# First group's attention in pairs of heads, with the low word of the weights on GpSimd

## The chip, the cores and the metric

One core of one Trainium2 chip runs the whole program. The metric is the device time of one execution in microseconds; lower is better. Three executions of the kernel before took 725.34, 726.88 and 729.34 us, a median of 726.88.

## The reference

Causal attention over 2 batches of 8 heads with 576 positions and head size 64, with a bias from cumulative sums; then two feed-forward layers over the 1152 tokens.

```python
scores = scale * (q @ k.T);  cum = cumsum(max(s, 0))
bias = -(cum[q] - cum[k])
scores = where(causal, -1e9, scores + min(bias, 0))
attn = softmax(scores);  x = attn @ v          # (1152, 512)
h = x @ w_in                                   # layer 1: 512 -> 2048
g = where(h > 0, h, exp(min(h, 0)) - 1);  x = g @ w_out
p = domain_probs / sum(domain_probs)           # layer 2: 4 experts, 512 -> 1024 -> 512
out = sum_e p[:, e] * (max(x @ w1[e], 0) @ w2[e])
```

The weights of layer 1 arrive as 64-bit floating-point numbers. The kernel takes them as pairs of 32-bit words and puts each number together from its high and its low word.

## The kernel before

**Tokens** come in three groups of 256, 448 and 448. For the first group the program runs its attention, then layer 1, then layer 2. The attention of the second group is cut into small parts, which are fed as background work into the end of the first group's layer 1 and into its layer 2. Then comes layer 1 of the second group with the attention of the third beside it, layer 1 of the third, and layer 2 of both.

**Layer 1** has 16 units of weights. A unit is 128 columns of `w_in` and 128 rows of `w_out`, 1 MB in 64-bit form. `layer1` (L648) makes one slot per unit: `up1` (four products into a PSUM bank, then the activation function in two ScalarE operations, L680 and L683, and one VectorE operation, L684, which writes the tile `gt`), and `down1` (four products, L663), two slots later. `slot` (L596) also calls the background work and `advance` (L573). `advance` decodes ahead (`AHEAD`), fetches and prepares the units that follow (layer 2's first unit is unit 16; `prepare`, L95, splits it into a high part on ScalarE, L99, and a low part on VectorE, L83).

**Decoding.** A unit has two halves, 32 halves in all. `fetch_halves` (L118) fetches a half (512 KB) by SP's queue into whatever buffer is free in a list of places (`turn`, L106): the tiles `wu`, `gt`, `yh`, `yl`, `raw`, `xa` and `ox` that later work will use. The first 16 halves find free places; each later one waits for a decode to free its place. `decode_halves` (L131) does per half one ScalarE operation on the high word (L146), one ScalarE operation on the low word (L148, into `z`, two buffers), and two VectorE operations that join them (L149, L151). After the second half of a unit, GpSimd's queue writes the decoded unit to DRAM (`w_dec`, L154), from where the later groups read it.

**Attention of the first group** (`attention_first`, L236) takes all 8 heads at once. `cum_sums` makes the cumulative sums, `cum_parts` writes their rows to DRAM (`rows_d`) for the later groups, `cum_columns` their columns. The scores of all heads (16 products, L277, and 32 for the bias, L283 and L285) fill six PSUM banks. `probabilities` takes a bank: per head a VectorE operation (L295, mask and row extreme) and an exponential on ScalarE (L297). `normalise` scales four heads, half on ScalarE (L304), half on VectorE (L305). `transposes` goes through PSUM and a ScalarE copy (L313), `values` multiplies by v, and a ScalarE copy (L322) writes `x_first`. Calls of `decode_halves` stand between: `DEC` has the number of halves that are decoded by each.

**Order.** The code is written in one sequence; a scheduler of the tile library then sets each engine's own order, by data dependences and its own estimates. Each engine and each DMA queue takes its instructions strictly in that order, so one that waits holds up all behind it. SP's queue carries nearly all loads, and the second group's first loads are tied to stand behind the last weight fetch (`late`, L525).

## Time and profile before

| | us |
|---|---|
| median of three runs | 726.88 |
| the profiled execution's own time | 726.64 |
| its span, first to last instruction | 724.8 |
| TensorE busy (share of the span) | 693.3 (96%) |
| VectorE busy | 559.1 (77%) |
| ScalarE busy | 371.7 (51%) |
| GpSimd busy | 13.6 (2%) |

Busy time is an average over stages that differ: a TensorE that is busy for 96% can still stand idle for a large part of one stage. So the stages are read apart, by windows of time. In a timeline a row begins with the start and the duration; a bracket at its end gives the idle time of the engine ahead of it and what ended that. Instructions of one engine may overlap a little, so the step from one start to the next is the better measure of a rate. PE is TensorE, DVE is VectorE, ACT is ScalarE, POOL is GpSimd; SPq is the queue that SP issues DMAs from.

### The profile page before, as it was taken

Reading aid. Unit: us, or ns where it says so; the run is one execution under the profiler, and the core shown is the slowest. Engines: PE = TensorE matmul, PEld = TensorE weight load, DVE = VectorE, ACT = ScalarE, POOL = GpSimd, SP = SyncE. Lnnn points to the kernel's source line nnn. Section 1 sums busy time; section 2 is a strip of 40 time slices with the busy share of each in tenths; the row PEclk is TensorE's granted clock in tenths of the full one; section 3 lists DMA queues with packets and bytes.
Section 4 is the critical chain, followed back from the end, with each engine's and each line's share of the span. In section 5 each row is a group of like instructions: output and inputs, shape, how many; then the busy total and the mean of one; then the engine's idle time right before and its main releaser. Section 6 shows DMA issues by size and latency. Waiting matters only on the chain.

```text
span 724.8 us, 10238 instructions
## 1 busy us (share of the span) xinstructions
PE 693.3 (96%) x3626; PEld 591.7 (82%) x3626; DVE 559.1 (77%) x1142; ACT 371.7 (51%) x777; POOL 13.6 (2%) x33
## 2 busy tenths in 40 slices
PE   5489789999999999999999999999999999999997
PEld 4378678888878888778899988888888888888886
DVE  4678659988875998886795549988888887887765
ACT  3978658776765878666744333222222222332320
POOL 2011000000000000000000000000000000000000
PEclk9599999999999999999999999999999999999999
DMA  8769994667556453441552000111111111111002
GB/s 325 301 237 368 327 319 160 207 198 216 167 188 203 166 158 108 145 141 59 213 222 88 30 0 1 59 58 59 59 58 59 59 58 59 58 59 59 0 1 101
DMA packets 41954, 96.98 MB, mean 134 GB/s; under 512 B 5200, under 2 KB 18704, under 8 KB 41904
## 3 DMA queue, kind: packets, MB, share of 16 engines
q1 hardware_dynamic: 39440, 87.69, 36.5%
q0 software_dynamic: 2304, 8.39, 2.9%
q8 instruction: 28, 0.46, 0.3%
q10 hardware_dynamic: 160, 0.26, 0.1%
q14 instruction: 22, 0.18, 0.1%
HBM read 85.32 MB, written 11.01 MB: 133 GB/s over the span
## 4 chain that ended last, share of the span: by engine, by line
PE 87%; ACT 4%; DMA 3%; DVE 3%; SPq 2%; issue 1%; DVEq 0%; ACTq 0%
PE acc L562 38%; PE up L562 16%; PE att L882 11%; PE up L882 8%; PE att L517 3%; PE att L490 3%; PE acc L663 2%; PE up L676 2%; PE att L445 1%; PE att L438 1%; SPq L370 1%; PE att L440 1%; DMA wu<-in_w 1%; DMA raw<-in_w 1%; DMA q<-in_qT 1%
## 5 line engine op out<-in xcount | busy, mean ns | idle before, releaser
L562 PE MATMUL acc<-w,h 128*128 128x512 f32 x672 | 172.0, 392 | 0.0
L562 PEld LDWEIGHTS acc<-w,h 128*128 128x128 f32 x672 | 126.1, 188 | 23.0 <-ACT h L892 0.2
L83 DVE TENSOR_TENSOR wu<-raw,wu 128x1024 fp32r<-128x1024 f32 x64 | 78.2, 1222 | 22.9 <-ACT wu L99 21.7
L562 PE MATMUL acc<-gt,wu 128*128 128x448 f32 x384 | 88.6, 373 | 0.0
L630 DVE SCALAR_TENSOR_TENSOR ox<-acc,pr,ox 128x512 f32<-128x512 f32 x105 | 78.6, 748 | 10.7 <-PE acc L562 8.6
L892 ACT ACTIVATE h<-c 128x448 fp32r<-128x448 f32 x48 | 27.4, 574 | 114.7 <-DVE c L898 114.7
L99 ACT ACTIVATE wu<-raw 128x1024 fp32r<-128x1024 f32 x64 | 67.5, 1055 | 22.4 <-PE acc L562 16.5
L562 PEld LDWEIGHTS acc<-gt,wu 128*128 128x128 f32 x384 | 70.1, 188 | 8.7 <-issue 2.6
L882 PE MATMUL att<-S,top 128*128 128x448 f32 x288 | 66.3, 365 | 0.0
L882 PEld LDWEIGHTS att<-S,top 128*128 128x128 f32 x288 | 54.0, 188 | 6.7 <-issue 0.2
L562 PE MATMUL acc<-wu,gt 128*128 128x512 f32 x192 | 56.4, 409 | 0.0
L562 PE MATMUL up<-yh,wu 128*128 128x256 f32 x256 | 52.6, 287 | 0.0
L893 DVE SCALAR_TENSOR_TENSOR h<-c,h 128x448 fp32r<-128x448 f32 x48 | 29.9, 624 | 18.7 <-ACT h L892 18.7
L882 PE MATMUL up<-x2a,top 128*128 128x448 f32 x192 | 44.2, 366 | 0.0
L562 PEld LDWEIGHTS up<-yh,wu 128*128 128x128 f32 x256 | 41.9, 190 | 2.7 <-issue 1.7
L562 PE MATMUL up<-xa,wu 128*128 128x448 f32 x192 | 43.6, 371 | 0.0
L562 PE MATMUL up<-ox,wu 128*128 128x448 f32 x192 | 42.1, 368 | 0.7 <-DVE e L688 0.7
L480 ACT ACTIVATE p<-p,nm 128x384 f32<-128x384 f32 (+4 forms) x56 | 34.5, 617 | 13.6 <-DVE nm L475 13.4
L680 ACT ACTIVATE e<-up 128x448 f32<-128x448 f32 (+1 forms) x48 | 23.5, 490 | 33.7 <-PE up L562 31.7
L882 PEld LDWEIGHTS up<-x2a,top 128*128 128x128 f32 x192 | 35.9, 188 | 4.8 <-ACT p L907 0.5
L562 PEld LDWEIGHTS up<-ox,wu 128*128 128x128 f32 x192 | 36.0, 188 | 4.6 <-DVE e L688 1.1
L892 ACT ACTIVATE h<-up 128x448 fp32r<-128x448 f32 x16 | 8.8, 547 | 58.1 <-PE up L882 58.1
(186 smaller groups left out, 1217.8 us busy)
## 6 DMA issues: line engine op xcount, KB each, us to landing
raw<-in_w SPq DMA_DIRECT2D x41, 512.0 KB
raw<-w_dec SPq DMA_DIRECT2D x32, 512.0 KB
raw<-in_w SPq DMA_DIRECT2D x16, 1024.0 KB
w_dec<-wu POOLq DMA_DIRECT2D x16, 512.0 KB, 6.7
k<-in_kT SPq DMA_DIRECT2D x16, 288.0 KB
xa<-in_w SPq DMA_DIRECT2D x6, 512.0 KB
ox<-in_w SPq DMA_DIRECT2D x6, 512.0 KB
cbp<-cum_d SPq DMA_DIRECT2D x16, 144.0 KB
```

What stands on the lines that cost most here:

```text
L83: DVE.tensor_tensor(out=lo, in0=x, in1=hi.bitcast(F32), op=ALU.subtract)
L99: ACT.activation(t[:, 0], x, AF.Copy)
L480: ACT.activation(p, p, AF.Exp, bias=nm, scale=-1.0, accum_out=sm)
L490: PE.transpose(pt[:cb[c + 1] - cb[c], m, :], p[:, cb[c]:cb[c + 1]], ident)
L517: PE.matmul(o[64 * j:64 * j + 64, qs:nq], job["v"][:n, c, 64 * j:64 * j + 64], job["pt"][:n, j, c, qs:nq], start=c == 0, stop=c == n_c - 1)
L562: PE.matmul(o, a[m], b[n], start=first and i == 0, stop=last and i == 2)
L630: DVE.scalar_tensor_tensor(out=o_sb, in0=o, scalar=pr[:, i, e:e + 1], in1=o_sb, op0=ALU.mult, op1=ALU.add)
L663: PE.matmul(o, t[:, 512 + 128 * c:640 + 128 * c], gt, start=k == 0, stop=k == NAB - 1)
L680: ACT.activation(e, o, AF.Exp)
L882: PE.matmul(bank, tops[q][:, m, op, cs], x[:, n, c], start=first and c + i == 0, stop=c == 1 and i == 2, skip_group_check=True)
L892: ACT.activation(h[:, 0, u, cs], c, AF.Relu)
L893: DVE.scalar_tensor_tensor(out=h[:, 1, u, cs], in0=c, scalar=0.0, in1=h[:, 0, u, cs].bitcast(F32), op0=ALU.max, op1=ALU.subtract)
```

## The change

1. `attention_first` works by pairs of heads (`hp` = 0 to 3). Each head has one PSUM bank for both its chunks. Scores of three pairs are made first, those of the fourth after the first pair's probabilities; then probabilities, normalising, transposes and values of the pairs follow each other as a pipeline. q and k are loaded in two halves each.
2. `normalise` scales everything on VectorE.
3. The low word of a half is taken by a multiplication on GpSimd instead of ScalarE's copy with a scale.
4. `DEC` is 1, 2, 3, 4 instead of 2, 5, 8, 10, and `AHEAD` 6 instead of 8: fewer halves are decoded during the attention, and less far ahead afterwards.
5. `cum_parts` and `cum_columns` are called in slot 3 of layer 1 instead of within and right after the attention.

```diff
-DEC = [2, 5, 8, 10]
-AHEAD = 8
+DEC = [1, 2, 3, 4]
+AHEAD = 6
...
-            ACT.activation(z, low.bitcast(U32), AF.Copy, scale=7.49 / 2 ** 32)
+            POOL.tensor_scalar(z, low.bitcast(U32), 7.49 / 2 ** 32, None, op0=ALU.mult)
...
     def cum_sums():
-        SP.dma_start(out=s_sb, in_=s)
...
+    def cum_parts():
+
         ACT.dma_start(out=cum_d, in_=cum)
-
-    def cum_parts():
-
...
-        cum_sums()
-        SP.dma_start(out=qkv[:, 0], in_=qT[0, :, 0:n].rearrange("(c p) n -> p c n", p=128))
-        SP.dma_start(out=qkv[:, 1], in_=kT[0, :, 0:n].rearrange("(c p) n -> p c n", p=128))
-        fetch_halves(2)
+        SP.dma_start(out=s_sb, in_=s)
+        for c in (0, 2):
+            for i, t in enumerate((qT, kT)):
+                SP.dma_start(out=qkv[:, i, c:c + 2], in_=t[0, 128 * c:128 * c + 256, 0:n]
+                             .rearrange("(c p) n -> p c n", p=128))
+        fetch_halves(1)
...
+        chunks = [(0, 128), (128, 256)]
+        banks = {}
+
+        def scores(hp):
+            for j in range(2):
+                h = 2 * hp + j
+                banks[h] = ps(f"acc{h % 4}", 1) if h < 4 or h > 5 else ps("up", 2)
...
+        def probabilities(hp):
+            for j in range(2):
+                h = 2 * hp + j
+                for i, (d0, d1) in enumerate(chunks):
+                    p = pp[h][:, d0:d0 + d1]
+                    nm = sb([128, 1], "nm", 8)
+                    DVE.tensor_tensor_reduce(p, banks[h][:, d0:d0 + d1], mask[:, S - d1:],
+                                             -1.0 / SC, 3.0e38, ALU.add, ALU.min, nm)
+                    ACT.activation(p, p, AF.Exp, bias=nm, scale=-1.0, accum_out=sm[:, i, h:h + 1])
+
+        def normalise(hp):
+            r = sm[:, :, 2 * hp:2 * hp + 2]
             DVE.tensor_scalar(r, r, 1e-9, None, op0=ALU.add)
             DVE.reciprocal(r, r)
-            for h in range(h0, h0 + 4):
-                ACT.activation(pp[h][:, 128:], pp[h][:, 128:], AF.Copy, scale=sm[:, 1, h:h + 1])
-                DVE.tensor_scalar(pp[h][:, :128], pp[h][:, :128], sm[:, 0, h:h + 1], None,
-                                  op0=ALU.mult)
...
+            for h in (2 * hp, 2 * hp + 1):
+                for i, (d0, d1) in enumerate(chunks):
+                    p = pp[h][:, d0:d0 + d1]
+                    DVE.tensor_scalar(p, p, sm[:, i, h:h + 1], None, op0=ALU.mult)
...
+        for hp in range(3):
+            scores(hp)
         probabilities(0)
+        decode_halves(DEC[0])
+        scores(3)
         probabilities(1)
-        decode_halves(DEC[0])
+        normalise(0)
+        transposes(0)
         probabilities(2)
+        normalise(1)
+        transposes(1)
+        values(0)
+        decode_halves(DEC[1])
         probabilities(3)
...
-    cum_columns(0, 4)
-    cum_columns(1, 4)
...
+    def sums_hook(k):
+        if k == 3:
+            cum_parts()
+            cum_columns(0, 4)
+            cum_columns(1, 4)
+
+    yacc = layer1(0, x_first, background, sums_hook)
```

What the scheduler makes of it is read from each engine's order.

ScalarE's order from the write of the cumulative sums to the first exponentials (L297 before, L301 after the change), where the sums' rows, the decoding and the attention meet. `bias` first holds `s` and later a row of ones. Before:

```order
L192 DMA cum_d<-cum 16x576
L202 ACTIVATE rows<-cum 16x576
L148 ACTIVATE z_246<-wu 128x512
L205 DMA rows_d<-rows 16x1152
L262 ACTIVATE cump<-cum 16x256
L262 ACTIVATE cumm<-cum 16x256
L199 DMA rows_d<-bias 16x576 x2
L202 ACTIVATE rows<-cum 16x576
L146 ACTIVATE wu<-wu 128x512
L148 ACTIVATE z_251<-wu 128x512
L205 DMA rows_d<-rows 16x1152
L297 ACTIVATE k_137,sm_142<-k_137,nm 128x128 x2
```

With the change:

```order
L193 DMA cum_d<-cum 16x576
L200 ACTIVATE rows<-cum 16x576
L203 DMA rows_d<-rows 16x1152
L263 ACTIVATE cump<-cum 16x256
L263 ACTIVATE cumm<-cum 16x256
L197 DMA rows_d<-bias 16x576 x2
L301 ACTIVATE k_138,sm_143<-k_138,nm 128x128
L301 ACTIVATE k_138,sm_143<-k_138,nm 128x256
```

The low words (L148) are gone, the second `rows` (L202, now L200) has moved behind nine exponentials, and the DMAs of `cum_d`, of the first `rows` and of the ones have stayed ahead of the first exponential.

VectorE's order in layer 1, two slots: L149 and L151 are the two joining operations of a half, L684 (L692 with the change) writes a slot's gated tile `gt`. Before, from the third gated tile on:

```order
L684 SCALAR_TENSOR_TENSOR gt<-up,e 128x256
L149 SCALAR_TENSOR_TENSOR wu<-wu,z_466 128x512
L151 SCALAR_TENSOR_TENSOR wu<-xa,wu 128x512
L149 SCALAR_TENSOR_TENSOR wu<-wu,z_506 128x512
L151 SCALAR_TENSOR_TENSOR wu<-ox,wu 128x512
L684 SCALAR_TENSOR_TENSOR gt<-up,e 128x256
L149 SCALAR_TENSOR_TENSOR wu<-wu,z_496 128x512
L151 SCALAR_TENSOR_TENSOR wu<-xa,wu 128x512
L149 SCALAR_TENSOR_TENSOR wu<-wu,z_532 128x512
L151 SCALAR_TENSOR_TENSOR wu<-ox,wu 128x512
L684 SCALAR_TENSOR_TENSOR gt<-up,e 128x256
```

With the change, from the first gated tile on:

```order
L692 SCALAR_TENSOR_TENSOR gt<-up,e 128x256
L213 COPY cum_t_97<-att 128x16
L149 SCALAR_TENSOR_TENSOR wu<-wu,z_381 128x512
L149 SCALAR_TENSOR_TENSOR wu<-wu,z_387 128x512
L151 SCALAR_TENSOR_TENSOR wu<-gt,wu 128x512
L151 SCALAR_TENSOR_TENSOR wu<-yh,wu 128x512
L692 SCALAR_TENSOR_TENSOR gt<-up,e 128x256
L149 SCALAR_TENSOR_TENSOR wu<-wu,z_404 128x512
L149 SCALAR_TENSOR_TENSOR wu<-wu,z_413 128x512
L151 SCALAR_TENSOR_TENSOR wu<-yl,wu 128x512
L151 SCALAR_TENSOR_TENSOR wu<-raw,wu 128x512
L692 SCALAR_TENSOR_TENSOR gt<-up,e 128x256
```

There are two halves a slot in both. Ahead of the first gated tile stand 4 halves' L149 with the change, where 11 stood before.

ScalarE's order near the end of the first layer 1: L680 and L683 (L688 and L691) are a slot's activation function, L426, L427 and L429 (L434, L435 and L437) split the next group's q and k, which wait for its loads, and L99 is the high part of layer 2's units. Before, from the activation function of the 14th slot on:

```order
L99 ACTIVATE wu<-raw 128x1024
L680 ACTIVATE e<-up 128x256
L683 ACTIVATE e<-e 128x256
L99 ACTIVATE wu<-raw 128x1024
L680 ACTIVATE e<-up 128x256
L683 ACTIVATE e<-e 128x256
L426 ACTIVATE qs<-pt 128x128
L427 ACTIVATE kh<-pt 128x128
L429 ACTIVATE qb<-pt 64x128
L480 ACTIVATE p,sm<-p,nm 128x128
```

With the change, from that of the 15th slot on:

```order
L688 ACTIVATE e<-up 128x256
L691 ACTIVATE e<-e 128x256
L99 ACTIVATE wu<-raw 128x1024
L434 ACTIVATE qs<-pt 128x128
L435 ACTIVATE kh<-pt 128x128
L437 ACTIVATE qb<-pt 64x128
L488 ACTIVATE p,sm<-p,nm 128x128
L688 ACTIVATE e<-up 128x256
L99 ACTIVATE wu<-raw 128x1024
L691 ACTIVATE e<-e 128x256
```

The first of layer 2's units stood ahead of the 14th slot's activation function and stands behind the 15th's; the second stands between the two operations of the 16th.

## Rows read from the trace of the kernel before

**Rows 1.** Busy time by windows, the sum of 105 to 724.8 us.

```profile
sum 619.80, PE 614.99 PEld 525.89 DVE 489.94 ACT 297.80 POOL 0.00; mean PE 205.00 PEld 175.30 DVE 163.31 ACT 99.27 POOL 0.00
```

**Rows 2.** Timeline of PE: start, duration, instruction, records, idle before.

```profile
6.43 4.34 PE L277 MATMUL acc<-pt 64*128 64x128 f32 x23 [6.43 <-DMA pt<-in_kT]
...
36.73 0.82 PE L312 MATMUL att<-ident,q 128*128 128x128 f32 x6
...
61.25 1.89 PE L676 MATMUL up<-xf,wu 128*128 128x256 f32 x8
...
64.70 1.89 PE L676 MATMUL up<-xf,wu 128*128 128x256 f32 x8
...
82.43 3.68 PE L676 MATMUL up<-xf,wu 128*128 128x256 f32 x8 [3.76 <-DVE gt L684]
...
104.95 0.47 PE L562 MATMUL up<-yh,wu 128*128 128x256 f32 x1
```

**Rows 3.** Timeline of ACT up to the first exponential.

```profile
8.43 0.67 ACT L148 ACTIVATE z<-wu 128x512 int32<-128x512 uint32 x1 [2.73 <-DMA wu<-in_w]
...
13.16 0.68 ACT L202 ACTIVATE rows<-cum 16x576 fp32r<-16x576 f32 x1 [3.46 <-DMA rows_d<-rows]
...
16.65 0.40 ACT L297 ACTIVATE k<-k,nm 128x128 f32<-128x128 f32 x1 [1.69 <-DVE nm L295]
```

**Rows 4.** Timeline of DVE: gated tiles (L684) and joining operations.

```profile
43.40 0.75 DVE L684 SCALAR_TENSOR_TENSOR gt<-up,e 128x256 f32<-128x256 f32 x2
...
65.39 0.42 DVE L684 SCALAR_TENSOR_TENSOR gt<-up,e 128x256 f32<-128x256 f32 x1
65.73 0.68 DVE L151 SCALAR_TENSOR_TENSOR wu<-xa,wu 128x512 int32<-128x512 int32 x1
66.33 0.69 DVE L149 SCALAR_TENSOR_TENSOR wu<-wu,z 128x512 int32<-128x512 int32 x1
...
69.06 0.42 DVE L684 SCALAR_TENSOR_TENSOR gt<-up,e 128x256 f32<-128x256 f32 x1
```

**Rows 5.** Timeline of SP's issues, then of ACT, 60 to 116 us.

```profile
62.81 5.33 SPq L127 DMA_DIRECT2D raw<-in_w  x3
...
90.17 0.33 SPq L93 DMA_DIRECT2D raw<-in_w  x1
...
80.84 0.31 ACT L429 ACTIVATE qb<-pt 64x128 fp32r<-64x128 f32 x1 [5.21 <-DMA pt<-in_qT]
...
96.85 1.06 ACT L99 ACTIVATE wu<-raw 128x1024 fp32r<-128x1024 f32 x1 [2.67 <-DMA raw<-in_w]
```

**Rows 6.** Busy time by windows, 90 to 105 us: PE, PEld, DVE, ACT, POOL, PEclk, DMA share, GB/s.

```profile
90.00:105.00 15.00, 12.96 (x62) 10.54 (x61) 8.95 (x27) 7.89 (x24) 1.06 (x2) 1.00 1.06 316
```

**Rows 7.** Groups by line and form, 0 to 105 us: busy us, mean ns | idle us before.

```profile
L148 ACT ACTIVATE z<-raw 128x512 int32<-128x512 uint32 x9 | 6.1, 698 | 1.3 <-DVE wu L149 1.3
...
L83 DVE TENSOR_TENSOR wu<-raw,wu 128x1024 fp32r<-128x1024 f32 x2 | 2.5, 1225 | 4.9 <-ACT wu L99 4.9
...
L295 DVE CUSTOM_DVE_ANT_0 k<-acc,mask 128x256 f32<-128x256 f32 x4 | 1.5, 419 | 0.0
...
L295 DVE CUSTOM_DVE_ANT_0 k<-acc,mask 128x128 f32<-128x128 f32 x6 | 1.4, 285 | 0.0
...
L305 DVE TENSOR_SCALAR k<-k,sm 128x128 f32<-128x128 f32 x6 | 1.4, 297 | 0.1
```

**Rows 8.** Timeline of POOL and DVE, 1.5 to 5.2 us.

```profile
1.50 0.29 POOL masks.py:199 TENSOR_SCALAR_AFFINE_SELECT ident<-ident 128x128 f32<-128x128 f32 x1
...
3.12 0.19 POOL L259 CAST ones<-ident 16x16 fp32r<-16x16 f32 x1
...
3.24 1.34 DVE L191 TENSOR_TENSOR_SCAN cum<-bias 16x576 f32<-16x576 f32 x1 [3.24 <-ACT bias L190]
3.37 1.41 POOL L261 CAST cump<-zero 64x256 fp32r<-64x256 f32 x1
...
4.74 0.39 POOL L261 CAST cumm<-zero 64x256 fp32r<-64x256 f32 x1
```

More of the change, by code (lines that the diff above doesn't have):

```diff
@@ L279, in attention_first @@
-        for (heads, i, tag), o in zip(banks, scores):
-            d0, d1 = 128 * i, 128 * i + 128
-            for n_, h in enumerate(heads):
-                one = ones[:, h:h + 1]
-                PE.matmul(o[:, n_], one.to_broadcast([80, 128]), parts[:, 0:d1],
-                          start=False, stop=False, skip_group_check=True)
-                PE.matmul(o[:, n_], less[:, d0:d1], one.to_broadcast([80, d1]),
-                          start=False, stop=n_ == len(heads) - 1, skip_group_check=True)
@@ L287, in attention_first @@
-        cum_parts()
-        def probabilities(bank):
-            heads, i, _ = banks[bank]
-            d0, d1 = 128 * i, 128 * i + 128
-            for n_, h in enumerate(heads):
-                p = pp[h][:, d0:d0 + d1]
-                nm = sb([128, 1], "nm", 8)
-                DVE.tensor_tensor_reduce(p, scores[bank][:, n_], mask[:, S - d1:], -1.0 / SC,
-                                         3.0e38, ALU.add, ALU.min, nm)
-                ACT.activation(p, p, AF.Exp, bias=nm, scale=-1.0, accum_out=sm[:, i, h:h + 1])
@@ L299, in normalise @@
-        def normalise(h0):
-            r = sm[:, :, h0:h0 + 4]
+        chunks = [(0, 128), (128, 256)]
[4 more added lines that the diff above has]
+                banks[h] = ps(f"acc{h % 4}", 1) if h < 4 or h > 5 else ps("up", 2)
+            for d0, d1 in chunks:
+                for j in range(2):
+                    r = slice(64 * j, 64 * j + 64)
+                    PE.matmul(banks[2 * hp + j][:, d0:d0 + d1], qkv[r, 0, hp, d0:d1],
+                              qkv[r, 1, hp, 0:d1], start=d0 == 0, stop=False,
+                              skip_group_check=True)
+            for j in range(2):
+                h = 2 * hp + j
+                one = ones[:, h:h + 1]
+                for d0, d1 in chunks:
+                    o = banks[h][:, d0:d0 + d1]
+                    PE.matmul(o, one.to_broadcast([80, 128]), parts[:, 0:d1],
+                              start=False, stop=False, skip_group_check=True)
+                    PE.matmul(o, less[:, d0:d1], one.to_broadcast([80, d1]),
+                              start=False, stop=d0 > 0, skip_group_check=True)
@@ new lines, in probabilities @@
+        def probabilities(hp):
+            for j in range(2):
+                h = 2 * hp + j
+                for i, (d0, d1) in enumerate(chunks):
[4 more added lines that the diff above has]
+                    ACT.activation(p, p, AF.Exp, bias=nm, scale=-1.0, accum_out=sm[:, i, h:h + 1])
@@ L315, in values, with transposes @@
-        def values(hp, tag):
-            o = ps(tag, 1)
+            for h in (2 * hp, 2 * hp + 1):
+                for i, (d0, d1) in enumerate(chunks):
+                    p = pp[h][:, d0:d0 + d1]
+                    DVE.tensor_scalar(p, p, sm[:, i, h:h + 1], None, op0=ALU.mult)
+        def transposes(hp):
+            for h in (2 * hp, 2 * hp + 1):
+                pt = ps_att()
+                for m in range(3):
+                    ms = slice(128 * m, 128 * m + 128)
+                    PE.transpose(pt[:, ms], pp[h][:, ms], ident)
+                ACT.activation(ptt[:, h], pt[:, :384], AF.Copy)
@@ L724, in tile_kernel @@
     n_tile = tok // 128
-    yacc = layer1(0, x_first, background)
+    def sums_hook(k):
[4 more added lines that the diff above has]
+    yacc = layer1(0, x_first, background, sums_hook)
     yh, yl = (sb([128, NCC, tok], t, 1, F32R) for t in ("yh", "yl"))
```

40 lines of the change are left out of this document (10 added, 30 removed).

## Prediction

> **What bounds the kernel now.** I read the busy table by windows first. From 105 us to the end TensorE is busy for 615.0 of 619.8 us [rows 1], so nothing there can take or give much, and whatever moves the 105 us mark moves the end by the same amount. The mark is the first product of the second layer, at 104.95 [rows 2]; it closes the first group's attention (to 43.4) and its first layer. The question is therefore where the change puts that mark.
>
> ScalarE's timeline tells what the attention waits for. ScalarE stands 2.73 us for a weight half so that it can take its low word, and 3.46 us because the second `rows` tile needs the buffer that a DMA to `rows_d` still reads; only then, at 16.65, does the first exponential start [rows 3]. On TensorE the scores were begun at 6.43 [rows 2]. Then decoding competes with attention on ScalarE and VectorE, and VectorE starts on the first gated tile at 43.40 [rows 4].
>
> In the first layer a slot is one up and one down product. TensorE alone needs 3.45 us for it (61.25 to 64.70) [rows 2], but the gated tiles come every 3.67 us (65.39 to 69.06) [rows 4]: ScalarE and VectorE set the pace. Later DMA does. The last weight fetches are issued from 62.81 to 68.14, held by buffers that decoding frees. The next group's loads stand behind them, and ScalarE waits 5.21 us for the first of these, until 80.84; TensorE then stands 3.76 us [rows 2, 5]. Unit 17's fetch is issued at 90.17, when a decode frees its buffer, and ScalarE starts on it at 96.85 [rows 5]; in this stretch the DMA engines are full (share 1.06) [rows 6].
>
> **The change, part by part.** I call `g(n)` the moment when VectorE starts on slot n's gated tile, n from 0 to 15; g(0) is 43.40 now.
>
> *Start.* The low word leaves ScalarE, and with it the 2.73 us wait. In the order the second `rows` stands after nine exponentials, so its 3.46 us wait is covered by them. 16.65 - 2.73 - 3.46 puts the first exponential at 10.5 and its reduction some 0.6 earlier, at 9.9. Dropping the first decode as well would allow still less, but the scores can't be ready much before: half of q and k should arrive before 6.43, at about 5, and 12 of 16 products come first. Asked to move `cum_parts` behind the attention, the scheduler leaves `cum_d`, the first `rows` and three of the four `rows_d` DMAs where they were. "Made afterwards" holds for the second `rows_d` write alone; the `rows_d` loads that wait for it on SP stand just before the 17th fetch, whose buffer isn't free until about g(1). I cost that at nothing.
>
> *Middle.* ScalarE loses about ten low words (0.70 each [rows 7], a little less where they follow each other), seven high words and eight scalings, some half of what it does up to 40 us. VectorE becomes the longer engine: 16 reductions (8 x 0.42 + 8 x 0.29 = 5.7), 16 scalings at 0.30 (4.8, some 0.4 more for the wide ones [rows 7]), 8 small operations at 0.2 (1.6), four halves of two operations at 0.60 (4.8): 17.3 us. Neighbours overlap by some 0.07 us [rows 4], which I leave in as allowance for waits on exponentials. The tail, from the last transposes to the gated tile, takes 36.73 to 43.40 now [rows 2, 4]; without three decoding operations on ScalarE it is about 5. So g(0) = 9.9 + 17.3 + 5 = 32.2: **11 us earlier**. Bounds: 30 (no waits) to 35 (TensorE slower after its gaps: eight records took 3.68 us after the 3.76 us one, else 1.89 [rows 2]).
>
> *What it defers.* Only 4 halves are decoded by g(0), against 11. Later the order has 2n+4 halves ahead of g(n), against 2n+7. Weight buffers come free in this order, so much of the 11 us is not passed on to DMA.
>
> *GpSimd's price.* Nothing in the trace multiplies on GpSimd. The nearest rows are its casts: 0.19 us for 16 columns, 0.39 for 256, so 0.83 ns per column, and 512 columns cost 0.19 + 496 x 0.83 = **0.60 us**. The other end is the mask operation, 0.29 us for 128 columns; if all of that grows with size, 512 cost 1.16 us [rows 8]. I take 0.60: the cast is also one input, one output and a change of type.
>
> *Who stands in whose way.* The same cast took 1.41 us while VectorE's scan ran, and 0.39 right after; it ended 0.2 us after the scan did [rows 8]. So GpSimd waited for a VectorE instruction with two inputs in SBUF, and each of the four decoding operations of a slot is one. If GpSimd's two operations find gaps of VectorE and only delay their own readers, the slot is 4 x 0.60 + 2 x 0.60 = 3.60 us, the gated operation (0.34 [rows 4]) being covered. If none overlaps, it is 2.74 + 1.20 = 3.94. I take the middle, **3.8 us** a slot. The Trainium skill (SBUF — State Buffer, Who interferes with whom) says that a VectorE instruction with two SBUF inputs and a GpSimd instruction that reads SBUF exclude each other for a whole instruction, whoever comes second. The row shows GpSimd's side; by the rule VectorE would wait just as well, and the slot would be the 3.94.
>
> *DMA and the end.* Let P be the slot. The last weight fetch needs half 20, which is decoded before g(9), less 1.3 for the operations between; with 0.5 to issue it goes out at 32.2 + 9 x 3.8 - 0.8 = 65.6, now at 68.14. The next group's first load then lands as much earlier: at 78.3 instead of 80.84, or g(9) + 11.9. ScalarE asks for it ahead of slot 12, at about g(11) + 0.9, so it waits 11 - 2P = 3.4 us. Hence g(14) = 32.2 + 14P + 11 - 2P = 43.2 + 12P = 88.8. Half 30, half a microsecond before, frees the buffer of unit 17: fetch at 88.3, landing 6.7 us later as now (90.17 to 96.85) at 95.0. Behind it in the order stand its high part (1.06 [rows 5]), low part (1.2 [rows 7]) and the last gated tile (0.4): 97.7. One down product (1.73, half of 3.45) and about 1 us of background follow: 100.4. The mark moves from 104.95 to 100.4, **4.6 us**. The profiled execution itself took 726.64, close to the median of 726.88, so the forecast is **722.0 us**.
>
> SP's four smaller q and k loads carry the bytes of two; the descriptors on POOL for `w_dec` (one a slot, now behind two multiplications) have slack in a slot.
>
> **Rivals.**
> 1. *VectorE is not slowed* (GpSimd takes the turns VectorE leaves). Then TensorE's 3.45 us paces. g(14) = 43.2 + 41.4 = 84.6, the mark is at 96.2, the time 717.9. For it: VectorE would have 0.7 us free in a slot. Against it: the cast that waited [rows 8].
> 2. *The DMA tail stays where it is*: the loads land at the same time because bandwidth, not release, sets them. ScalarE starts on unit 17 at 96.85, and 2.7 + 2.7 us later the mark is at 102.2: 724.0, within the noise. For it: share 1.06. Against it: before, SP waits for buffers that decoding frees; the last three issues took 5.33 us [rows 5].
> 3. *GpSimd becomes the bound, slower than before.* Place: the shared slot of VectorE and GpSimd, 14 slots long. With z us per multiplication P = 2.74 + 2z without overlap. The mark is back at 104.95 when g(14) is 93.4, P = 4.18, so z = 0.72; each further 0.1 us costs 12 x 0.2 = 2.4 us. At the far bound, 1.16, P = 5.06, g(14) is 103.9 and the mark 115.5: 737.2. For it: strided input, two type changes. Against it: the cast's row. The Trainium skill (GPSIMD Engine Reference, Elementwise — side-by-side cycle accounting) gives 769 ns measured for a tight one-input loop over 512 elements; no run here shows it. By that figure P is 4.28 and the time about 728, no change.
>
> That the change doesn't do what it says holds for the sums' rows only, and was costed above.
>
> **How the numbers follow.** A measurement of this kernel tells a difference of 0.5%, 3.6 us, from none. Chances: forecast 0.42, rival 1 0.16, rival 2 0.20, rival 3 0.22. The forecast is 1 us from that limit, so I give three quarters of it to faster; with rival 1 and a fifth of rival 2 that is 0.52. Same: a quarter of the forecast, most of rival 2 and a little of rival 3, 0.30. Slower: most of rival 3, 0.18. The range runs from 716, rival 1 with g(0) at 30, to 732, a slot of 4.6 us (z of 0.94). The forecast's own range, a slot of 3.60 to 3.94 and g(0) at 30 to 35, is 718 to 727.
>
> **What would show it.** First exponential near 10.5; g(0) near 32; GpSimd's multiplications near 0.6 us when alone and longer beside VectorE's decoding, and these beyond 0.69 us; g(n) every 3.8 us; ScalarE waiting about 3 us on the next group's first load; the second layer's first product near 100. It is wrong if the multiplication takes over 0.72 us, if slots keep 3.45 us, or if unit 17 still lands at 96.8.

## The result, and the profile after

The changed kernel takes **735.11 us**, median of 9 runs (732.41 to 736.49), where the kernel before takes 726.58 beside it (9 runs, 723.95 to 730.38): a ratio of 1.010, 95% interval 1.008 to 1.012. It is slower by 1%, outside the range of the forecast, and on the side of the third rival. The profiled execution took 735.11 as well, with a span of 731.6 (before 726.64 and 724.8).

TensorE's timeline has the mark. Columns here and below: start, duration, instruction, records, idle time before and what ended it.

```profile
4.92 2.93 PE L280 MATMUL acc<-pt 64*128 64x128 f32 x16 [4.92 <-DMA pt<-in_kT]
...
106.04 3.38 PE L671 MATMUL acc<-gt,wu 128*128 128x256 f32 x8
...
108.86 0.77 PE L570 MATMUL up<-yh,wu 128*128 128x256 f32 x1
...
116.78 0.51 PE L570 MATMUL up<-yh,wu 128*128 128x256 f32 x2 [0.76 <-DVE wu L83]
```

The scores begin at 4.92 (6.43 before), but the second layer's first product, the mark, comes at 108.86, 3.9 us **later** than the 104.95 of [rows 2]. The eight records in front of it took 3.38 us, where eight take 1.89 in [rows 2]. VectorE's timeline tells where an early start was lost.

```profile
33.65 0.69 DVE L149 SCALAR_TENSOR_TENSOR wu<-wu,z 128x512 int32<-128x512 int32 x1 [3.29 <-ACT wu L146]
...
34.98 0.42 DVE L692 SCALAR_TENSOR_TENSOR gt<-up,e 128x256 f32<-128x256 f32 x1
...
41.49 1.17 DVE L151 SCALAR_TENSOR_TENSOR wu<-raw,wu 128x512 int32<-128x512 int32 x1
...
42.58 0.41 DVE L692 SCALAR_TENSOR_TENSOR gt<-up,e 128x256 f32<-128x256 f32 x1
...
45.13 0.69 DVE L149 SCALAR_TENSOR_TENSOR wu<-wu,z 128x512 int32<-128x512 int32 x1 [1.42 <-POOL z L148]
...
47.41 0.41 DVE L692 SCALAR_TENSOR_TENSOR gt<-up,e 128x256 f32<-128x256 f32 x1
...
84.11 0.41 DVE L692 SCALAR_TENSOR_TENSOR gt<-up,e 128x256 f32<-128x256 f32 x1
```

The first gated tile (now L692) is written from 34.98 on, 8.4 us before the 43.40 of [rows 4]. But the next ones don't follow every 3.67 us: here it is 4.83 (42.58 to 47.41), and from slot 0 (34.98) to slot 14 (97.93) the mean is **4.50 us** (4.47 over the eleven slots up to 84.11, ahead of ScalarE's wait for the next group), where the forecast had 3.8. In such a slot VectorE stands 1.4 us for `z` from GpSimd, and the joining operation at 41.49 takes 1.17 us instead of the 0.68 of [rows 4]. Now GpSimd's own timeline:

```profile
9.92 1.51 POOL L148 TENSOR_SCALAR z<-wu 128x512 int32<-128x512 uint32 x1 [4.80 <-DMA wu<-in_w]
...
11.49 0.57 POOL L195 MEMSET bias<- 16x576 f32 x1
...
38.66 1.58 POOL L148 TENSOR_SCALAR z<-raw 128x512 int32<-128x512 uint32 x1
...
40.97 4.13 POOL L148 TENSOR_SCALAR z<-raw 128x512 int32<-128x512 uint32 x2
...
45.16 0.59 POOL L154 DMA_DIRECT2D w_dec<-wu  x1
...
45.83 4.09 POOL L148 TENSOR_SCALAR z<-xa 128x512 int32<-128x512 uint32 x2
```

One multiplication takes **1.51 us** where VectorE leaves it alone (9.92; 1.58 at 38.66) and 2.05 beside VectorE's decoding (two in 4.13). Two of these and the issue of `w_dec` (0.59), with the gaps, are 4.86 us from 40.97 to 45.83: GpSimd sets the slot. It is busy for 75.0 us up to the mark, 13.6 in the whole program before.

Later steps, ScalarE first and then SP's queue; the first answers to [rows 3], the others to [rows 5]:

```profile
12.09 0.78 ACTq L197 DMA_DIRECT2D rows_d<-bias  x2
...
12.92 0.40 ACT L301 ACTIVATE k<-k,nm 128x128 f32<-128x128 f32 x1 [5.34 <-DVE nm L299]
...
82.40 0.51 ACT L437 ACTIVATE qb<-pt 64x128 fp32r<-64x128 f32 x2 [3.48 <-DMA pt<-in_qT]
...
102.79 1.06 ACT L99 ACTIVATE wu<-raw 128x1024 fp32r<-128x1024 f32 x1 [2.08 <-DMA raw<-in_w]
...
114.41 1.06 ACT L99 ACTIVATE wu<-raw 128x1024 fp32r<-128x1024 f32 x1 [1.29 <-DMA raw<-in_w]
...
68.79 5.15 SPq L127 DMA_DIRECT2D raw<-in_w  x3
...
97.55 0.34 SPq L93 DMA_DIRECT2D raw<-in_w  x1
...
108.34 0.94 SPq L93 DMA_DIRECT2D raw<-in_w  x2
```

The first exponential starts at 12.92 (16.65 before), behind ScalarE's issue of the DMAs of the ones at 12.09 (ACTq is the queue that ScalarE issues DMAs from). The last weight fetches leave from 68.79 on (62.81), ScalarE's wait for the next group's first load is 3.48 us long and ends at 82.40 (80.84), and unit 17 is there at 102.79 (96.85). Units 18 and 19 are asked for at 108.34 (101.64 in the trace of before). Behind the mark some 3 us more are lost; by windows (busy us of PE, PEld, DVE, ACT, POOL, then TensorE's clock, DMA share, GB/s):

```profile
105.00:110.00 5.00, 4.09 (x14) 3.44 (x15) 3.80 (x14) 2.34 (x8) 0.00 (x0) 0.66 1.10 262
...
115.00:120.00 5.00, 3.98 (x26) 2.92 (x24) 3.93 (x12) 3.27 (x10) 0.00 (x0) 1.00 0.24 92
```

From 105 to 110 the granted clock is 0.66 after the wait in front (a mean of TensorE's two levels), and from 115 to 120 TensorE is idle for 1.0 us, 0.76 of it at 116.78, for unit 18's low part. So a mark that is 3.9 us late ends 6.8 us late.

### The profile page after: what moved, and what is told of

It reads as the page before. It is cut to its first block, busy times and chain, and to the rows that moved or that the text cites. A ratio compares the mean times of both kernels' runs of the same rounds, so it can differ in the third digit from the quotient of the medians.

```text
span 731.6 us, 10312 instructions
## 1 busy us (share of the span) xinstructions
PE 701.8 (96%) x3626; PEld 593.0 (81%) x3626; DVE 568.1 (78%) x1154; ACT 351.5 (48%) x737; POOL 75.0 (10%) x65
## 4 chain that ended last, share of the span: by engine, by line
PE 84%; DMA 5%; DVE 3%; POOL 3%; issue 2%; SPq 2%; ACT 1%; ACTq 0%; DVEq 0%; POOLq 0%
PE acc L570 38%; PE up L570 16%; PE att L895 10%; PE up L895 8%; PE att L525 3%; PE att L498 3%; POOL z L148 2%; PE att L453 1%; PE att L446 1%; DMA v<-in_v 1%; DVE wu L151 1%; PE att L448 1%; DMA q<-in_qT 1%; DMA wu<-in_w 1%; DMA xa<-in_w 1%
## 5 line engine op out<-in xcount | busy, mean ns | idle before, releaser
L99 ACT ACTIVATE wu<-raw 128x1024 fp32r<-128x1024 f32 x64 | 67.5, 1055 | 24.3 <-PE acc L570 16.2
L688 ACT ACTIVATE e<-up 128x448 f32<-128x448 f32 (+1 forms) x48 | 23.5, 489 | 56.6 <-PE up L570 31.7
L684 PE MATMUL up<-xf,wu 128*128 128x256 f32 x128 | 32.5, 393 | 12.0 <-DVE gt L692 11.1
L488 ACT ACTIVATE p<-p,nm 128x384 f32<-128x384 f32 (+4 forms) x56 | 34.5, 617 | 13.1 <-DVE nm L483 12.9
```

The lines of the kernel that those rows point to most:

```text
L99: ACT.activation(t[:, 0], x, AF.Copy)
L488: ACT.activation(p, p, AF.Exp, bias=nm, scale=-1.0, accum_out=sm)
L684: PE.matmul(o, t[:, dm(c)], x[:, c], start=c == 0, stop=c == NCC - 1)
L688: ACT.activation(e, o, AF.Exp)
```

## The experiments

Each is compared with the kernel before on the same chip. Theory A is the third rival: GpSimd's length is the loss. Its rival, B, is the smaller lead of decoding (`DEC`, `AHEAD`) or the order by pairs.

**E1: the low word back on ScalarE, the rest of the change kept.**

```diff
-            POOL.tensor_scalar(z, low.bitcast(U32), 7.49 / 2 ** 32, None, op0=ALU.mult)
+            ACT.activation(z, low.bitcast(U32), AF.Copy, scale=7.49 / 2 ** 32)
```

> The changed kernel with the low word back on ScalarE; the pipeline by pairs, the later sums and the smaller lead of decoding stay. Theory A (GpSimd is the whole loss: its multiplication takes 1.51 us alone and 2.05 beside VectorE's decoding, and VectorE waits 1.4 us a slot for it): the slot goes back to about 3.7 us as before (3.67), the first gated tile stays near 35, so slot 14 is at 35 + 11 + 12 x 3.67 = 90, the second layer's first product near 102 and the time near 723 to 725. Theory B (the lead of decoding, 2n+4 halves where it was 2n+7, or the order by pairs holds the first layer back, and GpSimd is only the wait that ends last): slots stay over 4.2 us and the time at 730 or more.

Measured: 726.17, ratio 0.998 (0.996 to 1.000). So the loss is gone, and B is wrong. But the mark came even earlier than expected and the time did not follow it:

```profile
70.72 0.42 DVE L692 SCALAR_TENSOR_TENSOR gt<-up,e 128x256 f32<-128x256 f32 x1
...
80.98 0.42 DVE L692 SCALAR_TENSOR_TENSOR gt<-up,e 128x256 f32<-128x256 f32 x1
...
77.45 0.31 ACT L437 ACTIVATE qb<-pt 64x128 fp32r<-64x128 f32 x1 [5.00 <-DMA pt<-in_qT]
...
97.21 0.47 PE L570 MATMUL up<-yh,wu 128*128 128x256 f32 x1
...
106.41 0.39 PE L570 MATMUL up<-yh,wu 128*128 128x256 f32 x1 [1.15 <-ACT wu L99]
...
99.75 0.35 SPq L93 DMA_DIRECT2D raw<-in_w  x1
```

The mark is 7.7 us before [rows 2], the span (721.9) 2.9 shorter. Between the gated tiles of slots 11 and 12 lie 10.3 us, in which ScalarE waits for the next group's first load. The last two lines, TensorE's wait for unit 18 behind the mark and that unit's fetch, are taken up below the table at the end of this section. This opened a second question, that of E12 to E18.

**E2: the other way round, the kernel before with the low word on GpSimd.** Its diff is E1's, reversed.

> The kernel before with the low word alone moved to GpSimd. Theory A: GpSimd needs 2 x 2.05 + 0.6 = 4.7 us for the two halves of a slot where 3.67 were enough, but 11 halves are decoded in the attention, so 7 or 8 of the slots wait fully: 5 to 10 us slower, 732 to 737. Theory B: the old lead of 11 halves covers GpSimd, 725 to 729.

Measured: 734.15, ratio 1.010 (1.008 to 1.012): as slow as the whole change. The mark is at 112.89. A again; the multiplication alone makes the loss.

**E3: only every second half on GpSimd.**

```diff
+            if part:
                 POOL.tensor_scalar(z, low.bitcast(U32), 7.49 / 2 ** 32, None, op0=ALU.mult)
+            else:
+                ACT.activation(z, low.bitcast(U32), AF.Copy, scale=7.49 / 2 ** 32)
```

> The changed kernel with every second half's low word (the first half of a unit) back on ScalarE, so that a slot has one multiplication of each engine. Theory A: GpSimd has 2.05 + 0.6 = 2.65 us in a slot and is no bound; VectorE loses some 0.5 us a slot to one multiplication instead of two, so the slot is 3.7 or less, the mark 101 to 103 and the time 722 to 725. Theory B: 730 or more, like the changed kernel.

Measured: 725.09, ratio 0.997 (0.995 to 0.999). A's case: with one multiplication a slot GpSimd is no bound. The mark comes 3.0 us before that of [rows 2], and here the span, 721.5, is 3.3 shorter:

```profile
101.92 0.78 PE L573 MATMUL up<-yh,wu 128*128 128x256 f32 x1
```

**E4: GpSimd writes zeros** (`POOL.memset(z, 0)` in the multiplication's place).

> The changed kernel with GpSimd writing zeros in place of the multiplication: the low word of the first layer's weights is left out, GpSimd's operation reads nothing from SBUF. Theory A with the exclusion lying in GpSimd's read: VectorE's decoding operations stay at 0.6 to 0.7 us, none at 1.1, the slot goes to TensorE's 3.45 to 3.6 us, the second layer's first product comes at 96 to 99 and the time is 717 to 721. If writes are excluded as well, some of VectorE's operations stay at 1 us. Theory B: slots over 4.2 us, 730 or more.

Measured: 722.27, ratio 0.992 (0.990 to 0.995). Groups by line and form (busy us, mean ns | idle before), first both joining operations, then GpSimd's:

```profile
L149 DVE SCALAR_TENSOR_TENSOR wu<-wu,z 128x512 int32<-128x512 int32 x32 | 20.7, 684 | 6.6 <-ACT wu L146 6.4
...
L151 DVE SCALAR_TENSOR_TENSOR wu<-raw,wu 128x512 int32<-128x512 int32 x9 | 5.9, 682 | 0.0
...
L148 POOL MEMSET z<- 128x512 int32 x32 | 17.0, 534 | 47.5 <-DVE wu L149 46.5
```

None of VectorE's joining operations takes over 0.69 us, as alone, beside 32 operations of GpSimd. What stood in VectorE's way was GpSimd's **read**. It also answers for the start: the first exponential is at 10.72 here and at 12.92 with the multiplication. There GpSimd's `memset` of the ones (11.49 above) stands behind its first multiplication, which waits for the weights until 9.92, and ScalarE's DMAs of the ones follow at 12.09. The wait counts for more than the price: with the cast of E11 the first exponential is at 12.57.

**E5 and E10: the price of GpSimd's forms**, in a stretch put ahead of the program (128x512 throughout):

```diff
+        lo, c = t[:, :, 0], t.rearrange("p a b -> p (a b)")[:, 512:]
+        POOL.tensor_scalar(o, lo.bitcast(U32), 7.49 / 2 ** 32, None, op0=ALU.mult)
+        POOL.tensor_scalar(o.bitcast(F32), c.bitcast(F32), 7.49, None, op0=ALU.mult)
+        POOL.tensor_copy(o, lo.bitcast(F32))
+        POOL.tensor_copy(o.bitcast(F32), c.bitcast(F32))
+        POOL.memset(o, 0)
```

> The changed kernel with a measured stretch ahead of the rest: GpSimd's multiplication of 128x512 in several forms (every second word or neighbouring words read, integers or floats, a copy, half the columns, a memset), each form alone, beside 24 VectorE operations with two SBUF inputs, and beside 24 with one. If the read of every second word makes the 1.51 us, neighbouring words take about half of it; if the change of type does, floats take half of it in either layout; if it is the plain price of a column, all stay near 1.5 us, and half the columns take 0.75. Beside VectorE's operations with two inputs each form that reads is longer by up to an operation of VectorE (0.6), and VectorE's by as much; beside operations with one input neither is.

> As e5, with the stretches kept apart by data: GpSimd's forms (multiplication of every second word twice, of neighbouring floats, a cast of every second word, a copy, a memset, 128x512 each) first beside nothing, then beside 16 VectorE operations with two SBUF inputs, then beside 16 with one. If only instructions with two inputs are excluded, VectorE's operations with one input keep the time that they have alone, and GpSimd's multiplication there keeps 1.5 us; beside those with two, GpSimd's take 2.0 and some of VectorE's 1.1. If GpSimd's read stands in the way of every VectorE operation, both stretches show it.

GpSimd's timeline in E10, where VectorE leaves it alone, in the order of the diff:

```profile
7.44 1.52 POOL L184 TENSOR_SCALAR yh<-xf 128x512 int32<-128x512 uint32 x1
...
12.31 1.49 POOL L185 TENSOR_SCALAR yh<-xf 128x512 f32<-128x512 f32 x1
...
15.46 0.64 POOL L186 CAST yh<-xf 128x512 int32<-128x512 f32 x1
...
16.56 0.60 POOL L187 COPY yh<-xf 128x512 f32<-128x512 f32 x1
...
17.22 0.53 POOL L188 MEMSET yh<- 128x512 int32 x1
```

The multiplication takes 1.5 us for integers of every second word and for neighbouring floats alike. A cast takes 0.64, a copy 0.60, a `memset` 0.53. So neither the stride nor the type is dear, but the multiplication as such; in E5 256 columns took 0.86 where 512 took 1.49, some 2.5 ns a column, three times the 0.83 worked out for the casts. Beside VectorE the expectation that one input is harmless fell: the scalings of one input (L345) take 0.65 and 0.70 in E10 where they take 0.28 and 0.35 in E1, some of the operations of one input put there for it 0.69 to 0.83 where others of them take 0.41, and GpSimd's multiplications beside them 1.67 to 1.77. The scheduler mixed other VectorE operations into these stretches, so who waited for whom, one by one, is not settled by them. The Trainium skill (SBUF — State Buffer, Who interferes with whom) says that GpSimd's reads are in contention with VectorE's operations of two SBUF inputs, GpSimd's mere writes are not, and that VectorE's operations of one input are too where they run in a mode that uses two ports. The runs agree: two inputs and a read in E11, writes alone in E4, one input in E10, though no row names a mode or a port.

**E11: the price that the prediction took.** GpSimd copies a byte of each low word.

```diff
-            POOL.tensor_scalar(z, low.bitcast(U32), 7.49 / 2 ** 32, None, op0=ALU.mult)
+            top = x.rearrange("p a b -> p (a b)").bitcast(mybir.dt.uint8)
+            POOL.tensor_copy(z, top.rearrange("p (a b) -> p a b", b=8)[:, :, 3])
```

> The changed kernel with GpSimd copying the top byte of each low word (a cast, no arithmetic) in place of the multiplication: three mantissa bits of the first layer's weights are wrong, everything else is the change. This gives GpSimd the price that the prediction took, 0.60 to 0.65 us, and leaves its read of SBUF in place. If the prediction's other steps hold, the slot is 3.8, the second layer's first product near 100.4 and the time 722, some 0.6% under before. If reading beside VectorE is dear by itself, casts of 1.1 us and more than one VectorE operation of 1.1 in a slot make the slot 4.2 or more, and the time is 726 or more. If the stretch behind the mark takes the early start back, as in e1 (mark 97.2, end only 2.9 earlier), the mark is at 96 to 100 and the time 723 to 726.

Measured: 727.19, ratio 0.999 (0.997 to 1.001). Timelines of VectorE, GpSimd and TensorE:

```profile
58.39 1.28 DVE L150 SCALAR_TENSOR_TENSOR wu<-wu,z 128x512 int32<-128x512 int32 x2
...
59.60 1.14 DVE L152 SCALAR_TENSOR_TENSOR wu<-yh,wu 128x512 int32<-128x512 int32 x1
...
13.34 0.64 POOL L149 CAST z<-wu 128x512 int32<-128x512 uint8 x1 [1.63 <-DMA wu<-in_w]
...
59.14 2.12 POOL L149 CAST z<-raw 128x512 int32<-128x512 uint8 x2 [1.20 <-DVE wu L150]
...
101.69 0.47 PE L571 MATMUL up<-yh,wu 128*128 128x256 f32 x1
```

The cast takes 0.64 alone and 1.06 beside VectorE, whose second operation takes 1.14. The slot is 3.87 (34.64 to 77.25 for eleven), the mark 101.69, near the forecast's 3.8 and 100.4. But the time is that of before, not 722: even with the price that it took, the last step of the forecast would have failed.

**E6 to E9: more lead of decoding.** The diff is that of E7 (in E1), E8 (in the changed kernel) and E9 (in E3); E6 is E1 with `AHEAD = 8` alone.

```diff
-DEC = [1, 2, 3, 4]
-AHEAD = 6
+DEC = [2, 4, 6, 8]
+AHEAD = 10
```

> The changed kernel with the low word on ScalarE (as e1) and AHEAD 8 in place of 6, DEC as in the change. In e1 the second layer's first product came at 97.2, 7.7 us earlier than before, but the span was only 2.9 shorter; its DMA share was 0.39 and 0.34 from 30 to 40 us and near 1.03 from 45 to 80. Theory C (the stretch up to 105 us is bound by DMA, and its hole at 30 to 40, where decoding frees no buffers, is what is lost): two halves more decoded after the first gated tile fill a part of the hole, the next group's first load lands 1 to 3 us earlier than 77.45, and the time is 1 to 3 us under e1's, 723 to 725 beside 726 to 727 of before. Rival D (the lead costs the first gated tiles what it gives DMA): within 1 us of e1.

> As e6, with DEC [2, 4, 6, 8] and AHEAD 10: four more halves are decoded in the attention. They cost VectorE 4 x 1.3 us, so the first gated tile comes near 39 to 40 (34.17 in e1). Theory C: the hole of DMA is filled, the first load of the next group lands near 73, unit 17 near 89, and the time is 3 to 6 us under before, 720 to 723. Rival D: the later first gated tile moves all by 5 us, 726 to 730.

> The changed kernel, GpSimd's multiplication kept, with DEC [2, 4, 6, 8] and AHEAD 10. Theory A: GpSimd has the same 32 halves at 2.05 and 16 issues at 0.6 to do, 75 us, and is the bound whatever the lead, so the time stays within 2 us of the changed kernel, 733 to 737. Theory B (the smaller lead of decoding is what slows the changed kernel): 724 to 729.

> As e3 (one of a unit's two low words on GpSimd, one on ScalarE), with DEC [2, 4, 6, 8] and AHEAD 10. Theory C: as e7 or up to 2 us better, because ScalarE is relieved of half the low words: 718 to 723. If GpSimd's remaining 2.05 us a unit still hold decoding back in the attention, where halves follow closely, it is slower than e7 by 1 to 4 us.

Measured: E6 726.63, ratio 0.999 (0.998 to 1.000); E7 726.04, 0.998 (0.997 to 0.999); E8 738.66, **1.016** (1.014 to 1.017); E9 730.64, 1.004 (1.003 to 1.006). E8 is the last blow to B: with more lead the changed kernel is slower still, 1.7 us above A's own range. C did not come true by lead alone: E7 filled the hole at 35 to 40 us (share 0.98) and kept one at 80 to 85 (0.67; 0.58 in E1). Why E9 falls behind both E3 and E7 was not taken further; its first gated tile came at 40.95, 3.2 us after E7's.

**E12: ScalarE's wait moved behind the first layer**, in E1.

```diff
+            last_exp[0] = ACT.activation(e, o, AF.Exp)
...
+            with (tc.issue_after(last_exp[0].ins) if g == 1 else nullcontext()):
+                split(items[0])
...
-BG_FROM = [14, 0, 0]
+BG_FROM = [15, 0, 0]
```

> e1 (low word on ScalarE) with the next group's first split held back on ScalarE until the exponential of slot 15 has been issued, so that slots 12 to 15 don't stand behind ScalarE's wait for the next group's first load (5.0 us in e1, until 77.45; 10.3 us from the gated tile of slot 11 to that of slot 12). Theory E (this wait takes back e1's early start): the gap falls to 3.5, the second layer's first product comes at 91 to 94 and the time is 3 to 6 us under e1's. Theory F (DMA bandwidth sets when the layer-2 weights and the next group's heads are there, DMA share near 1 until 105 in both kernels): the mark moves earlier, TensorE waits behind it instead, and the time stays within 1.5 us of e1's.

Measured: 726.46, ratio 0.999 (0.997 to 1.000). E fell. The gated tiles of slots 11 and 12 are 3.7 us apart now (72.80 and 76.52), but TensorE then waits 5.7 us for slot 14, whose turn on ScalarE stands behind unit 16, asked for at 79.05 and there at 88.33. By windows:

```profile
30.00:40.00 10.00, 8.80 (x49) 6.62 (x48) 6.82 (x15) 9.56 (x21) 1.22 (x2) 1.00 0.23 94
...
40.00:60.00 20.00, 20.00 (x94) 17.62 (x93) 19.87 (x45) 18.72 (x38) 3.20 (x6) 1.00 1.01 376
...
60.00:75.00 15.00, 15.00 (x71) 13.20 (x70) 12.52 (x22) 12.48 (x25) 2.13 (x4) 1.00 1.02 416
...
85.00:90.00 5.00, 0.33 (x2) 0.00 (x0) 0.58 (x1) 1.64 (x3) 0.00 (x0) 1.00 1.04 391
90.00:95.00 5.00, 2.08 (x4) 1.18 (x4) 1.68 (x3) 1.90 (x6) 0.00 (x0) 0.50 1.05 290
```

The DMA engines (the last but one column) are full from 40 us on; only from 30 to 40 they are not. The mark, 101.16, is 4 us later than E1's, which neither theory had: one wait for loads took the place of another, and behind it TensorE runs at its lower level (granted clock 0.50, 1.2 GHz) from 90 to 100 us.

**E14, E15, E18: more bytes.** Four unused transfers of 512 KB, in E1 (E14) and in the kernel before (E15), and in E1 again at a set place (E18):

```diff
+                wd = POOL.dma_start(out=w_dec[n], in_=units[n])
+                if 4 <= n < 8:
+                    with tc.issue_after(wd.ins):
+                        POOL.dma_start(out=extra[n - 4], in_=w[n])
```

> e1 with four more transfers of 512 KB from DRAM to DRAM, issued with the decoded units 4 to 7, at some 45 to 55 us, used by nobody. At the 420 GB/s of the full stretches they take 5 us of all engines. Theory F: the DMA engines are full from 40 to 80 us in e1, so all that stands behind comes 5 us later, and the end 3 to 6 us later than e1's: 728 to 732. Theory G: within 1.5 us of e1's.

> The kernel before with the same four extra transfers, which fall at some 43 to 58 us, where its DMA share is 0.57 and 0.44. Theory F: half or more of them fit into the hole, so the end is 0 to 3 us later than before, less than e14 loses against e1. If DMA has slack everywhere, no change; if every byte counts, 5 us.

> As e14 (e1 with four unused transfers of 512 KB from DRAM to DRAM), each now issued only after the decoded unit 4, 5, 6, 7 has been sent, at some 43 to 55 us, so the attention stays as it is in e1 (first gated tile near 34 to 36). Theory F (DMA, full from 40 us on in e1, holds the end): the next group's first load lands 4 to 6 us after e1's 77.45, and the time is 3 to 6 us over e1's 726, ratio to before 1.002 to 1.007. Theory G (DMA has slack behind 40 us and the order of attention and products holds the end): ratio 0.996 to 1.000 as e1.

Measured: E14 732.82, ratio 1.009 (1.006 to 1.011); E15 731.37, 1.006 (1.004 to 1.008); E18 734.41, **1.009** (1.007 to 1.012). E14 and E15 missed their place: without the tie the transfers went out at 5 to 7 us, ahead of the first weights, and held the attention back too. E18 is clean, with its first gated tile at 35.00:

```profile
46.91 0.51 POOL L158 DMA_DIRECT2D extra<-in_w  x1
...
56.30 0.50 POOL L158 DMA_DIRECT2D extra<-in_w  x1
...
85.20 0.31 ACT L441 ACTIVATE qb<-pt 64x128 fp32r<-64x128 f32 x1 [4.93 <-DMA pt<-in_qT]
```

The next group's first load comes 7.75 us after E1's, the mark 11.5 later, and the span is 10.7 longer. F holds for the stage up to the mark: what is added to DMA from 47 us on comes out at the end, and more than the 3 to 6 us expected.

**E13, E16, E17: both holes filled.** E7 with E12's tie (E13), the kernel before with that tie alone (E16), and E13 with `DEC, AHEAD = [3, 6, 9, 11], 12` (E17).

> e7 (low word on ScalarE, DEC [2, 4, 6, 8], AHEAD 10) with the first split held back as in e12. e7 filled a part of DMA's hole at 30 to 40 us and kept one at 80 to 85 (share 0.67); e12 filled the one at 80 to 85 (1.04) and kept one at 30 to 40 (0.23). Theory F (DMA's total up to some 105 us holds the end): with both filled, DMA is done 3 to 5 us earlier and the time is 2 to 5 us under e1's, 721 to 724 where before is at 727. Theory E fell with e12. Theory G (the order of attention and products behind the mark holds the end, not DMA): 725 to 727 again.

> The kernel before with the first split held back as in e12 and nothing else. Theory F: the kernel before has holes of DMA at 30 to 40 us (share 0.47 and 0.62) and at 45 to 55 (0.57 and 0.44), 9 us in all, and its stretch from 55 on is full already, so holding the split gives nothing: within 1.5 us of before. If the held split is the whole gain of e13, 3 to 5 us under before.

> e13 with DEC [3, 6, 9, 11] and AHEAD 12 in place of [2, 4, 6, 8] and 10. e13's DMA share is 0.84 at 25 to 30 us and 0.48 at 30 to 35: some 3.4 us of hole. Theory F: if the earlier decodes fill half of it, 1 to 2 us under e13, 720 to 722. If they only move the first gated tile back by 4 us while the hole moves with it, as slow as e13 or 1 to 3 us slower.

Measured: E13 722.58, ratio **0.994** (0.992 to 0.997); E16 731.63, 1.006 (1.004 to 1.009); E17 722.84, 0.996 (0.994 to 0.997). E13 is the fastest that computes everything: low words on ScalarE, the pipeline by pairs, a lead near the old one, and the tie.

```profile
30.00:35.00 5.00, 4.99 (x29) 3.61 (x28) 3.72 (x9) 4.88 (x12) 0.89 (x2) 1.00 0.48 171
...
35.00:40.00 5.00, 2.29 (x11) 2.04 (x12) 4.96 (x13) 4.74 (x11) 1.06 (x2) 1.00 0.97 336
...
80.00:85.00 5.00, 3.72 (x16) 2.96 (x16) 2.60 (x5) 0.84 (x2) 1.06 (x2) 1.00 1.01 345
...
100.00:105.00 5.00, 5.00 (x41) 4.82 (x40) 3.18 (x11) 2.58 (x10) 0.00 (x0) 1.00 0.26 84
```

DMA's share is full again at 35 to 40 and at 80 to 85, and its work is done by 100 us (0.26 after it; 1.09 in the kernel before from 100 to 105). In the old kernel the tie alone costs time (no change was expected; why was not taken further), so E13's gain is not the tie's alone. E17 gains nothing over E13.

Taken together, from each profile (us; the mark is the second layer's first product):

| kernel | first gated tile | mark | span | span less mark |
|---|---|---|---|---|
| before | 43.40 | 104.95 | 724.8 | 619.9 |
| change | 34.98 | 108.86 | 731.6 | 622.7 |
| E2, multiplication alone | 42.91 | 112.89 | 733.6 | 620.7 |
| E3, every second half | 34.12 | 101.92 | 721.5 | 619.6 |
| E1, ScalarE | 34.17 | 97.21 | 721.9 | 624.7 |
| E11, cast | 34.64 | 101.69 | 727.6 | 625.9 |
| E4, no read | 31.52 | 95.06 | 722.6 | 627.5 |
| E7, lead | 37.77 | 100.68 | 722.7 | 622.0 |
| E12, tie | 35.93 | 101.16 | 724.8 | 623.6 |
| E13, lead and tie | 37.23 | 99.97 | 720.7 | 620.7 |
| E17, more lead and tie | 40.47 | 100.92 | 720.7 | 619.7 |

The last column would be one number if the mark carried the end. In E3 and E17 it is that of before: marks 3.0 and 4.0 us earlier came out at the end in full. In E1, E4 and E11 it is 5 to 8 us larger. These are single executions, and those of one kernel differ by up to 8 us (E1's spans run from 721.0 to 729.2), so the column alone proves little. The traces tell more. Where unit 18's fetch leaves 2 us or more ahead of the mark (3.3 in the kernel before, 3.1 in E7, 2.1 in E3), TensorE has no wait over 0.15 us in the 40 us behind the mark. In the change it leaves 0.5 ahead, and the waits add up to 1.0 us. In E4, E11 and E1 it leaves 0.3, 0.6 and 2.5 us behind the mark; the waits are 2.2 to 2.9 us (in E1 half of them for unit 18, in the others all), and TensorE then runs at a lower clock for a while (in E4 0.50 from 105 to 110 us and 0.60 from 110 to 115). E7's 622.0 comes without such waits and stays open.

## Why the prediction was wrong

**GpSimd's price: the step that failed first.** The forecast put the multiplication at 0.60 us, from the casts of [rows 8], "one input, one output and a change of type". It took 1.51. The casts' row was right for casts (0.64 in E10 and E11), but the nearest row was the other one, the mask operation, which also computes; and even that end, 1.16, was too low. The doubts that rival 3 held, a strided input and two changes of type, were not the reason either (E10). The 769 ns that the Trainium skill (GPSIMD Engine Reference, Elementwise — side-by-side cycle accounting) gives as the best case, a tight loop over 512 elements, is half of what this instruction measures.

**The slot.** The forecast had 3.8; over the eleven slots ahead of ScalarE's wait it measured 4.47. The rule that GpSimd and VectorE hold each other up was right (2.05 against 1.51, and 1.14 against 0.68 in E11), though not for the whole of a multiplication: no joining operation of the change takes over 1.17 us, 0.48 more than alone, beside multiplications of 2 us. E11's 3.87 with the assumed price falls between its bounds, 3.60 and 3.94. Rival 3's own sum for 1.51, 2.74 + 2 x 1.51 = 5.76, is too much: it lets nothing run together, while in the trace one of a slot's multiplications runs beside other work. GpSimd's queue, two operations and the issue, is what bounds it; that the issue for `w_dec` has "slack in a slot" fell with the price.

One reading of the kernel before was off as well: ScalarE and VectorE did not set the old pace. Busy time by windows there (PE, PEld, DVE, ACT, POOL, clock, DMA share, GB/s):

```profile
60.00:75.00 15.00, 15.00 (x71) 13.22 (x70) 12.37 (x21) 12.64 (x26) 2.13 (x4) 1.00 0.98 392
```

TensorE has no gap, and makes a slot's products in the 3.45 us of [rows 2]. The gated tiles, 3.67 us apart, were ready before TensorE came to them. So taking work off ScalarE could bring the products forward, but not make TensorE's own slot shorter than 3.45.

**The start** came within its bounds only just: the first gated tile at 34.98, 32.2 forecast, with bounds of 30 and 35. Two of its steps were wrong. The first exponential was forecast at 10.5 and came at 12.92, because the wait for the weights did not leave ScalarE with the low word: it reached it through GpSimd, the `memset` behind the first multiplication and the DMAs of the ones (10.72 in E4, where nothing waits for weights there). And VectorE was not the longer engine throughout: it waits 3.29 us for ScalarE's high word ahead of the last decoding (33.65).

**From the slot to the mark** the working came out close, in part by luck. With the measured 34.98 and 4.47, slot 14 is at 34.98 + 11 + 12 x 4.47 = 99.6, measured 97.93; with E11's numbers it is 34.64 + 11 + 12 x 3.87 = 92.1, measured 92.27. ScalarE's wait was forecast at 3.4 and was 3.48, but that is a coincidence: for a slot of 4.47 the working gives 11 - 2 x 4.47 = 2.1, and for E11's 3.3 where ScalarE waits 7.12 us, until 81.54.

**From the mark to the end: the second step that failed.** "Whatever moves the 105 us mark moves the end by the same amount" held in E3 and E17 and failed in E1, E4, E11 and the change itself. [rows 1] show TensorE full behind 105 us because the next units arrive just in time there; [rows 6], with DMA's share of 1.06, were the warning. Unit 18 is asked for at 101.64 in the kernel before, 99.75 in E1 and 102.25 in E11, on SP's queue behind the next group's loads. A mark that comes 7.7 us earlier (E1) then waits for it, runs slower behind the wait, and gives a span 2.9 shorter. That the fetch's lead over the mark decides is read from the traces; no run moved this one fetch alone. Rival 2's time, 724.0, is near what is measured once GpSimd is out of the way (E1 and E11, 726 and 727), but it does not come about as that rival has it: in E1 unit 17 is there at 92.86, not at 96.85, and the time is lost behind the mark. Rival 2 was taken to exclude the forecast's case, and the loads are a bound of their own.

**The sum.** The time is 13.1 us over the forecast. The mark is 8.5 later than its 100.4: 12 x (4.47 - 3.8) = 8.0 from the slot and 2.8 from the first gated tile, less 2.3 by which the working overstates slot 14 and what follows it. Behind the mark 2.9 are added: TensorE is idle for 1.3 us more there (622.7 less 616.6 busy, against 619.9 less 615.0), some 1.0 of it for unit 18, and the rest is longer busy time, of which the lower clock right behind the mark is a part that was not taken out. The last 1.7 lie outside the span: 735.11 less 731.6 is 3.5 us, 726.64 less 724.8 was 1.8.

## What to carry to other kernels

An idle engine is priced by its own row for the same kind of operation: a copy's row says nothing of a multiplication on GpSimd, and where no such row exists, the range has to reach well over the nearest one. Count an engine's operations per slot against the slot before counting what they free elsewhere: two at 2 us can't fit into 3.7. Before calling a mark the end's measure, look at what stands behind it: where DMA feeds the next stage, an earlier mark is worth only what the next loads also gain (E3 kept all of its 3.0 us, E1 2.9 of its 7.7). Here it took the filling of both holes to get 0.6% out of a first gated tile that was ready 6 to 9 us earlier.
